# Seven block products in place of eight in the first layer of a second MLP

## Chip, cores and metric

The kernel runs on one core of a Trainium2 chip (trn2). The metric is device time in microseconds of one execution. The kernel before was timed in three runs.

## What is computed

The program is a chain: attention with a cumulative bias (16 heads of 576 tokens and 64 channels), an MLP ("moe"), and a mixture of four MLPs ("moe2"). All is float32. The change lies in the third part:

```python
def _moe2_ref(x, domain_probs, w1, w2):         # x: 1152 x 512, w1: 4 x 512 x 1024, w2: 4 x 1024 x 512
    p = domain_probs / (domain_probs.sum(-1, keepdims=True) + 1e-09)
    out = np.zeros((N, D), dtype=np.float32)
    for e in range(E):
        h = np.maximum(x @ w1[e], 0.0)
        out += p[:, e:e + 1] * (h @ w2[e])
    return out.astype(np.float32)
```

## The kernel before

**Precision.** A float32 operand of the MLPs is held as a pair: `hi`, the value cast to fp32r, and `lo`, the rest. `products` (L150) makes one block product from three matmuls: weight hi by data hi, weight lo by data hi, weight hi by data lo. All of one tile add up in one PSUM bank.

**Stages.** The 1152 tokens lie in three chunks of 512, 320 and 320 (`sizes`). Phases 0, 1 and 2 run the first MLP on a chunk each; attention is woven into phases 0 and 1. Phase 3 runs the four second MLPs on all chunks. Its unit is a block: 4 tiles of 128 hidden channels of one expert, so 8 blocks in all. A block has

- an up part (`up`, L170): for each tile of hidden channels and each chunk one PSUM tile, of 4 steps over the 512 inputs by 3 matmuls. So 4 tiles x 12 matmuls of 512 columns, and 4 x 2 x 12 of 320. ACT writes `hi` of the hidden tile `ht` with Relu (L190), DVE `lo` (L191).
- a down part (`down2`, L216): for each of the 9 tiles of 128 tokens 12 matmuls of 512 columns; DVE scales by the expert's probability and adds to `oacc` (L228). `up` of the next block stands before and behind a block's `down2` (`in_order`, L119).

**Weights** come in pieces of 128x1024 float32 (512 KB): SP loads one into `raw` (4 buffers, `RAW`), ACT casts `hi` (L104), POOL subtracts for `lo` (L105), into one of 4 buffers `w`. The pieces of the first MLP arrive as 64-bit patterns; in phase 0 `convert` (L73) makes float32 of each in the `raw` buffer, with one ACT and four DVE instructions (L84 to L88). In phase 3 a block takes two up pieces and two down pieces.

**What sets the order.** Each engine has one queue, worked off in order. A scheduler that simulates the program places the instructions in it; pools of tiles with a fixed number of buffers hold an instruction back until a buffer is free. PSUM has 8 banks of 512 float32 columns: 3 for the MLPs in phases 0 to 2, 6 in phase 3 (`ps_all`). The outputs `y_t` of the first MLP are split into `hi` and `lo` as their tiles end (L212, L213).

Of the kernel before, what the change touches and what calls it, by code (L numbers as in the profile page):

```python
# [18 lines left out]
def attention_moe_moe2(ctx: ExitStack, tc: tile.TileContext, q, k, v, s, w_in, w_out, probs, w1, w2, out):  # L19
# [21 lines left out]
    RAW, SPLIT = 4, 4  # L41
    sizes = (512, 320, 320)
    starts = (0, 512, 832)

    const = ctx.enter_context(tc.tile_pool(name="const", bufs=1))
    ypool = ctx.enter_context(tc.tile_pool(name="ypool", bufs=1))
    rawp = ctx.enter_context(tc.tile_pool(name="rawp", bufs=RAW))
    xpool = ctx.enter_context(tc.tile_pool(name="xpool", bufs=1))
# [101 lines left out]
    def products(ps, pairs):  # L150

        pairs = [p for (wh, wl), (xh, xl) in pairs for p in ((wh, xh), (wl, xh), (wh, xl))]
        for i, (a, b) in enumerate(pairs):
            nc.tensor.matmul(ps, a, b, start=(i == 0), stop=(i == len(pairs) - 1))  # L154
# [15 lines left out]
    def up(e, chunks, h, tiles):  # L170

        nonlocal w_up
        x = x_t if e is None else y_t
        for i in tiles:
# [6 lines left out]
            for c, to, n in pieces(chunks):  # L181
# [3 lines left out]
                if e is None:  # L185
                    nc.scalar.activation(hi, ps, AF.Prelu, alpha=0.01)
                    nc.scalar.activation(ps, ps, AF.Prelu, alpha=0.01)  # L187
                    nc.vector.tensor_tensor(lo, ps, f32(hi), ALU.subtract)  # L188
                else:
                    nc.scalar.activation(hi, ps, AF.Relu)  # L190
                    nc.vector.scalar_tensor_tensor(lo, ps, 0.0, f32(hi), ALU.max, ALU.subtract)  # L191
                yield

    def down1(f, chunks, h, w):

        for c, to, n in pieces(chunks):
            if f == 0:
                yacc[c] = ypool.tile([P, KD, sizes[0]], F32, tag="yacc", name="yacc")[:, :, : sizes[c]]
            for d in range(KD):
# [4 lines left out]
                if f == 0:  # L204
                    nc.scalar.copy(ya, ps)
                else:
                    nc.vector.tensor_tensor(ya, ps, ya, ALU.add)  # L207
                if f + len(h) == DFF // P:
                    if d == 0:
                        y_t[c] = xpool.tile([P, 2, KD, sizes[c]], F32R, tag=f"x{c}", name=f"y{c}")  # L210
                    hi, lo = at(y_t[c], d)
                    nc.scalar.copy(hi, ya)  # L212
                    nc.vector.tensor_tensor(lo, ya, f32(hi), ALU.subtract)  # L213
# [325 lines left out]
```

## Time and profile before

| | us |
|---|---|
| median of the three timed runs | 762.21 |
| lowest and highest of them | 760.3 and 763.31 |
| span of the profiled execution | 762.5 |
| of it: PE busy | 739.5 (97%) |
| PE weight loads (PEld) busy | 651.3 (85%) |
| DVE busy | 322.3 (42%) |
| ACT busy | 301.9 (40%) |
| POOL busy | 266.1 (35%) |

The profile shows one execution, from its first to its last instruction; its span lies among the three timed runs. PE is TensorE's matmuls, PEld its weight loads, which overlap the matmuls. A row's mean duration is that of one instruction from start to end; neighbouring matmuls overlap, so the pace of a row of matmuls is not its mean but the time of many, less one, over their count. The granted clock of TensorE is 1.00 of full speed (2.4 GHz) from 113 us on.

### The profile page before, as it was taken

To read this page: it belongs to the slowest core of one execution; us is meant where nothing else is said; L and a number is where in the kernel's file an instruction comes from. 1 tells how busy PE (TensorE), PEld (TensorE's weight loads), DVE (VectorE), ACT (ScalarE), POOL (GpSimd) and SP (SyncE) were. 2 spreads that over 40 slices of the span, in tenths; PEclk is the share of its full clock that TensorE was granted. 3 is DMA by queue.
4 is the path that set the end of the run, shared out by engine and by line. 5 is a ranking of instruction groups with operands and counts; after the bars stand their busy time and mean duration, and the time that the engine had idled before them with its cause. 6 is when DMAs were issued, how large, how long until landed. Compare 5 with 4: busy or idle time off the path is not lost.

```text
span 762.5 us, 10790 instructions
## 1 busy us (share of the span) xinstructions
PE 739.5 (97%) x4140; PEld 651.3 (85%) x4140; DVE 322.3 (42%) x665; ACT 301.9 (40%) x613; POOL 266.1 (35%) x198
## 2 busy tenths in 40 slices
PE   7889999989999999999999999999999999999997
PEld 5677778867899999999998888988989889888886
DVE  4889666985564553223322222222222222222222
ACT  4766596565577574654320321212203112032010
POOL 3553164667376353676311221212203121122100
PEclk9789999999999999999999999999999999999999
DMA  7888946765242223445210110201001101010002
GB/s 241 231 254 290 323 155 217 209 217 178 97 142 99 89 84 110 140 139 166 69 41 28 56 56 0 84 28 56 28 28 60 53 32 51 28 28 1 0 29 96
DMA packets 45955, 80.74 MB, mean 106 GB/s; under 512 B 4528, under 2 KB 24496, under 8 KB 45904
## 3 DMA queue, kind: packets, MB, share of 16 engines
q1 hardware_dynamic: 45904, 80.06, 32.8%
q8 instruction: 32, 0.52, 0.3%
q14 instruction: 19, 0.16, 0.1%
HBM read 69.26 MB, written 10.78 MB: 105 GB/s over the span
## 4 chain that ended last, share of the span: by engine, by line
PE 84%; DVE 5%; DMA 5%; issue 2%; ACT 2%; SPq 1%; POOL 0%; ACTq 0%; DVEq 0%
PE ps_d L154 38%; PE ps_u L154 36%; PE ps_o L406 5%; PE ps_pt L397 2%; DMA r<-in_moe_w_out_dram 2%; DMA r<-in_moe_w_in_dram 2%; PE ps_sc L383 2%; PE ps_sc L380 1%; DVE raw L85 1%; DVE raw L88 1%; DMA pn<-in_moe_domain_probs_dram 1%; ACT raw L84 1%; DVE z L384 1%; DVE raw L87 1%; DVE raw L86 0%
## 5 line engine op out<-in xcount | busy, mean ns | idle before, releaser
L105 POOL TENSOR_TENSOR w<-raw,w 128x1024 fp32r<-128x1024 f32 x80 | 195.7, 2456 | 364.4 <-ACT w L104 361.7
L154 PE MATMUL ps_u<-y,w 128*128 128x320 f32 (+1 forms) x1152 | 201.5, 336 | 0.7 <-DVE yacc L207 0.7
L154 PEld LDWEIGHTS ps_u<-y,w 128*128 128x128 f32 x1152 | 185.2, 188 | 17.0 <-ACT w L104 0.9
L154 PE MATMUL ps_d<-w,ht 128*128 128x512 f32 x864 | 197.3, 389 | 0.0
L154 PEld LDWEIGHTS ps_d<-w,ht 128*128 128x128 f32 x864 | 161.9, 188 | 33.2
L104 ACT CAST w<-raw 128x1024 fp32r<-128x1024 f32 x80 | 83.1, 1044 | 170.0 <-issue 161.9
L191 DVE SCALAR_TENSOR_TENSOR ht<-ps_u,ht 128x320 fp32r<-128x320 f32 (+1 forms) x96 | 53.6, 558 | 146.8 <-ACT ht L190 146.8
L154 PE MATMUL ps_u<-x,w 128*128 128x320 f32 (+1 forms) x576 | 112.9, 343 | 1.7 <-DVE ht L188 1.7
L154 PE MATMUL ps_d<-ht,w 128*128 128x320 f32 (+1 forms) x576 | 110.3, 341 | 0.9 <-DVE ht L188 0.9
L190 ACT ACTIVATE ht<-ps_u 128x320 fp32r<-128x320 f32 (+1 forms) x96 | 47.2, 491 | 142.1 <-PE ps_u L154 142.1
L154 PEld LDWEIGHTS ps_u<-x,w 128*128 128x128 f32 x576 | 91.9, 189 | 9.0 <-DVE ht L188 2.3
L228 DVE SCALAR_TENSOR_TENSOR oacc<-ps_d,pn,oacc 128x512 f32<-128x512 f32 x63 | 47.3, 751 | 122.8 <-PE ps_d L154 122.8
L154 PEld LDWEIGHTS ps_d<-ht,w 128*128 128x128 f32 x576 | 92.2, 188 | 7.9 <-DVE ht L188 1.1
L406 PEld LDWEIGHTS ps_o<-vs,pv 128*128 128x128 f32 x480 | 64.4, 200 | 10.6 <-DVE xo L412 3.8
L406 PE MATMUL ps_o<-vs,pv 128*128 128x64 f32 x480 | 65.9, 277 | 3.8 <-DVE xo L412 2.4
L376 POOL TENSOR_SCALAR_AFFINE_SELECT nck<-nck 128x128 f32<-128x128 f32 x80 | 34.1, 441 | 85.8 <-DMA nck<-cum_d 37.7
L388 ACT ACTIVATE z<-z,mn 128x512 f32<-128x512 f32 (+4 forms) x80 | 48.4, 606 | 29.8 <-DVE mn L384 23.7
L384 DVE CUSTOM_DVE_ANT_0 z<-ps_sc,nck 128x512 f32<-128x512 f32 (+4 forms) x80 | 40.8, 511 | 32.1 <-PE ps_sc L383 18.9
L398 ACT COPY pv<-ps_pt 128x512 f32<-128x512 f32 (+3 forms) x96 | 39.2, 422 | 22.6 <-PE ps_pt L397 17.2
L380 PE MATMUL ps_sc<-kr,qz 128*128 128x128 f32 (+4 forms) x96 | 35.9, 470 | 8.3 <-DVE mn L384 7.9
L397 PE MATMUL ps_pt<-ident,z 128*128 128x128 f32 x240 | 42.0, 280 | 1.8 <-ACT pv L398 1.3
L188 DVE TENSOR_TENSOR ht<-ps_u,ht 128x320 fp32r<-128x320 f32 (+1 forms) x48 | 26.4, 553 | 36.0 <-ACT ps_u L187 35.8
(55 smaller groups left out, 440.6 us busy)
## 6 DMA issues: line engine op xcount, KB each, us to landing
raw<-w_f SPq DMA_DIRECT2D x32, 512.0 KB, 3.3
raw<-in_moe_w_dram SPq DMA_DIRECT2D x32, 512.0 KB, 3.5
r<-in_moe_w_in_dram SPq DMA_DIRECT2D x16, 512.0 KB, 6.9
w_f<-raw SPq DMA_DIRECT2D x16, 512.0 KB, 3.7
r<-in_moe_w_out_dram SPq DMA_DIRECT2D x16, 512.0 KB, 5.8
nck<-cum_d SPq DMA_DIRECT2D x8, 576.0 KB, 5.1
vs<-in_v_dram SPq DMA_DIRECT2D x12, 256.0 KB, 4.1
kr<-in_k_dram SPq DMA_DIRECT2D x8, 288.0 KB, 4.5
```

Of the source, the lines that this page charges most:

```text
L104: nc.scalar.copy(w[:, 0], raw)
L105: nc.gpsimd.tensor_tensor(w[:, 1], raw, f32(w[:, 0]), ALU.subtract)
L154: nc.tensor.matmul(ps, a, b, start=(i == 0), stop=(i == len(pairs) - 1))
L190: nc.scalar.activation(hi, ps, AF.Relu)
L191: nc.vector.scalar_tensor_tensor(lo, ps, 0.0, f32(hi), ALU.max, ALU.subtract)
L228: nc.vector.scalar_tensor_tensor(oacc[tt], ps, p, oacc[tt], ALU.mult, ALU.add)
L380: nc.tensor.matmul(ps, self.qz[:, j, own], self.kr[:, keys], start=True, stop=True)
L384: nc.vector.tensor_tensor_reduce(out=z[:, keys], in0=ps, in1=nck[:, j, keys], scale=-(D ** -0.5), scalar=3.0e38 if pc == 0 else mn[:, 0:1] ...
L388: nc.scalar.activation(z, z, AF.Exp, bias=mn[:, pc : pc + 1], scale=-1.0, accum_out=self.st[i][:, j : j + 1])
L397: nc.tensor.transpose(pt[:, (kt - k0) * P : (kt - k0 + 1) * P], z[:, tiles[kt][0] : tiles[kt][2]], ident)
L398: nc.scalar.copy(pv[:, k0:k1].rearrange("p t q -> p (t q)"), pt)
L406: nc.tensor.matmul(o[:, j], pv[:, kt], self.vs[:, kt, j], start=(kt == 0), stop=(kt == i))
```

## The change

The first layer of the second MLPs goes by Strassen's scheme (in Winograd's form). A product of a weight cut into 2x2 blocks (256 inputs by 128 hidden channels each) with tokens cut into 2x2 blocks (256 inputs by n tokens each) needs seven products of sums of blocks and not eight of the blocks. The tokens are paired in two sets: set 0 has the first 256 tokens of chunk 0 beside its last 256 (n = 256), set 1 has chunk 1 beside chunk 2 (n = 320).

- `seven` replaces the split of an up piece: DVE forms four sums of 128x256 in `sums`; ACT and POOL then split seven blocks (1792 columns, in three instructions each) and not four (1024). The two buffers `w7` and the one of `sums` have a pool of their own.
- `paired_tokens` forms the four sums of the token blocks (DVE) and splits seven blocks (ACT and DVE), once for each set, before the first block. `down1` adds the last tile of the first MLP straight into a float32 `y_t`, and no longer splits it.
- `up2` makes one pair of hidden tiles for one set: seven products of 6 matmuls each, into 4 PSUM banks. Three of the four banks are written, read by ACT or DVE, and then added onto by a second product. ACT copies `p1` (L264); DVE adds into `u2`, `u4` and three tiles of `mixed` (L266 to L275); then three Relu and three `lo` (L278, L279), of which two read `mixed` and no longer PSUM.
- `second` sets the order: the down tiles of set 0, one `up2` of the next block, the down tiles of set 1, three more `up2`.
- `RAW` falls from 4 to 3. Down pieces of phase 3 have two buffers (`wdown`), opened with the other pools of phase 3 when those of the first MLP close. PSUM has 8 banks in one pool in phase 3, where it had 6.

```diff
-    RAW, SPLIT = 4, 4
+    RAW, SPLIT = 3, 4
+    sets = (((0, 0), (0, 256), 256), ((1, 0), (2, 0), 320))
...
+    def seven(raw):
+        r = raw.rearrange("p (k f) -> p k f", k=KD)
+        a11, a12, a21, a22 = (r[:, 2 * j : 2 * j + 2, i * P : (i + 1) * P] for i in range(2) for j in range(2))
+        sums = w7pool.tile([P, 4, 2, P], F32, tag="sums", name="sums", bufs=1)
+        nc.vector.tensor_tensor(sums[:, 0], a21, a22, ALU.add)
+        nc.vector.tensor_tensor(sums[:, 1], sums[:, 0], a11, ALU.subtract)
+        nc.vector.tensor_tensor(sums[:, 2], a11, a21, ALU.subtract)
+        nc.vector.tensor_tensor(sums[:, 3], a12, sums[:, 1], ALU.subtract)
+        w = w7pool.tile([P, 2, 7, 2, P], F32R, tag="w7", name="w7", bufs=2)
+        for i, j, of in ((0, 2, r[:, :, :P]), (2, 3, a22), (3, 7, sums.rearrange("p s k f -> p (s k) f"))):
+            hi, lo = (w[:, l, i:j].rearrange("p s k f -> p (s k) f") for l in range(2))
+            nc.scalar.copy(hi, of)
+            nc.gpsimd.tensor_tensor(lo, of, f32(hi), ALU.subtract)
+        return w
...
-    def products(ps, pairs):
+    def products(ps, pairs, onto=False):
...
-            nc.tensor.matmul(ps, a, b, start=(i == 0), stop=(i == len(pairs) - 1))
+            nc.tensor.matmul(ps, a, b, start=(i == 0 and not onto), stop=(i == len(pairs) - 1), skip_group_check=onto)
...
+    def paired_tokens(s, pool):
...
+        nc.vector.tensor_tensor(sums[:, 1], b12, b11, ALU.subtract)
+        nc.vector.tensor_tensor(sums[:, 2], b22, sums[:, 1], ALU.subtract)
+        nc.vector.tensor_tensor(sums[:, 3], b22, b12, ALU.subtract)
+        nc.vector.tensor_tensor(sums[:, 0], b21, sums[:, 2], ALU.subtract)
+        y = y7[s] = pool.tile([P, 2, 7, 2, n], F32R, name=f"y7_{s}")
+        for i, j, of in ((0, 2, left), (2, 3, b22), (3, 7, sums.rearrange("p s k t -> p (s k) t"))):
+            hi, lo = (y[:, l, i:j].rearrange("p s k t -> p (s k) t") for l in range(2))
+            nc.scalar.copy(hi, of)
+            nc.vector.tensor_tensor(lo, of, f32(hi), ALU.subtract)
+
+    def up2(w, s):
...
+        bank = [ps_mm.tile([P, 512], F32, tag="mm", name=f"ps_u{i}")[:, :n] for i in range(4)]
+
+        def product(to, a, b, onto=False):
+            products(bank[to], [(at(w, a, k), at(x, b, k)) for k in range(2)], onto)
+
+        product(0, 0, 0)
+        nc.scalar.copy(p1, bank[0])
+        product(1, 4, 5)
+        nc.vector.tensor_tensor(u2, bank[1], p1, ALU.add)
+        product(2, 3, 4)
+        nc.vector.tensor_tensor(u4, bank[2], u2, ALU.add)
+        product(3, 5, 6)
+        nc.vector.tensor_tensor(mixed[:, 1], bank[3], u4, ALU.add)
+        product(0, 1, 1, True)
+        product(2, 6, 2, True)
+        nc.vector.tensor_tensor(mixed[:, 2], bank[2], u2, ALU.add)
+        product(3, 2, 3, True)
+        nc.vector.tensor_tensor(mixed[:, 0], bank[3], u2, ALU.add)
+        for of, f, cols in ((bank[0], 0, slice(0, n)), (mixed[:, 2], 0, slice(n, 2 * n)), (mixed[:, :2].rearrange("p i t -> p (i t)"), 1, slice(0, 2 * n))):
+            hi, lo = at(ht, f, cols)
+            nc.scalar.activation(hi, of, AF.Relu)
+            nc.vector.scalar_tensor_tensor(lo, of, 0.0, f32(hi), ALU.max, ALU.subtract)
+        return ht
...
+        for i, (e, *_) in enumerate(blocks):
+            wd = next_w(2)
+            down2(e, parts[0], h[i], wd)
+            if i + 1 < len(blocks):
+                up_part(i + 1, 0, 0)
+            down2(e, parts[1], h.pop(i), wd)
+            if i + 1 < len(blocks):
+                for pair, s in ((1, 0), (0, 1), (1, 1)):
+                    up_part(i + 1, pair, s)
...
+        paired_tokens(0, y7p)
         for _ in mlps(phases[2]):
             pass
...
+    paired_tokens(1, y7q)
+    first.close()
+    banks.close()
+    ps_mm = ctx.enter_context(tc.tile_pool(name="ps_all", bufs=8, space=PSUM))
+    wpool = ctx.enter_context(tc.tile_pool(name="wdown", bufs=2))
```

On PE, the up part of one block of phase 3 stands in a row before (`ps_u` is the PSUM tile, `y0` to `y2` the chunks, `w` the weight piece):

```order
L154 MATMUL ps_u_4556<-y0_2231,w_4409 128x512 x12
L154 MATMUL ps_u_4571<-y1_3456,w_4409 128x320 x12
L154 MATMUL ps_u_4586<-y2_4048,w_4409 128x320 x12
L154 MATMUL ps_u_4602<-y0_2231,w_4409 128x512 x12
L154 MATMUL ps_u_4617<-y1_3456,w_4409 128x320 x12
L154 MATMUL ps_u_4632<-y2_4048,w_4409 128x320 x12
```

These are the first two of the block's four hidden tiles. Now, on PE, the same block after the down tiles of set 1 (`y7_0` and `y7_1` are the token sums of the two sets, `ps_u0` to `ps_u3` the four banks of one `up2`):

```order
L177 MATMUL ps_u0_4635<-y7_0_3512,w7_4421 128x256 x6
L177 MATMUL ps_u1_4636<-y7_0_3512,w7_4421 128x256 x6
L177 MATMUL ps_u2_4637<-y7_0_3512,w7_4421 128x256 x6
L177 MATMUL ps_u3_4638<-y7_0_3512,w7_4421 128x256 x6
L177 MATMUL ps_u0_4695<-y7_1_4124,w7_4409 128x320 x6
L177 MATMUL ps_u1_4696<-y7_1_4124,w7_4409 128x320 x3
L177 MATMUL ps_u0_4635<-y7_0_3512,w7_4421 128x256 x6
L177 MATMUL ps_u1_4696<-y7_1_4124,w7_4409 128x320 x3
L177 MATMUL ps_u2_4637<-y7_0_3512,w7_4421 128x256 x6
L177 MATMUL ps_u3_4638<-y7_0_3512,w7_4421 128x256 x6
```

The second products onto banks 0, 2 and 3 stand behind nine or more matmuls of the next `up2`.

On DVE, the rows of the same stretch after the change (`tmp` holds `u2`, `u4` and `mixed`; L266, L268 and L270 free banks 1, 2 and 3 for it):

```order
L266 TENSOR_TENSOR tmp_4634<-ps_u1_4636,tmp_4634 128x256
L268 TENSOR_TENSOR tmp_4634<-ps_u2_4637,tmp_4634 128x256
L270 TENSOR_TENSOR tmp_4634<-ps_u3_4638,tmp_4634 128x256
L266 TENSOR_TENSOR tmp_4694<-ps_u1_4696,tmp_4694 128x320
L279 SCALAR_TENSOR_TENSOR ht_4633<-ps_u0_4635,ht_4633 128x256
L273 TENSOR_TENSOR tmp_4634<-ps_u2_4637,tmp_4634 128x256
L275 TENSOR_TENSOR tmp_4634<-ps_u3_4638,tmp_4634 128x256
L279 SCALAR_TENSOR_TENSOR ht_4633<-tmp_4634,ht_4633 128x256
L268 TENSOR_TENSOR tmp_4694<-ps_u2_4697,tmp_4694 128x320
L279 SCALAR_TENSOR_TENSOR ht_4633<-tmp_4634,ht_4633 128x512
L270 TENSOR_TENSOR tmp_4694<-ps_u3_4698,tmp_4694 128x320
```

Before, only the `lo` of each PSUM tile (L191) stood here. On ACT, the start of phase 3 after the change (`y2` is the last output of the first MLP, `w_4152` and `w_4217` the first two down pieces):

```order
L248 CAST y7_1_4124<-y1_3447 128x1280
L248 CAST y7_1_4124<-y2_4071 128x640
L264 COPY tmp_4156<-ps_u0_4157 128x256
L248 CAST y7_1_4124<-sums_4119 128x2560
L127 CAST w_4152<-raw_4150 128x1024
L278 ACTIVATE ht_4155<-ps_u0_4157 128x256
L127 CAST w_4217<-raw_4215 128x1024
L264 COPY tmp_4221<-ps_u0_4222 128x256
```

The copy that the second `up2` needs (`tmp_4221`) stands behind the cast of the token sums of set 1 and two casts of weights.

## Rows read from the trace of the kernel before

**Rows 1.** Busy time by stretch: start:end, length, then time (count) for each engine

```profile
core 0: us, PE busy (x) PEld busy (x) DVE busy (x) ACT busy (x) POOL busy (x), PEclk, DMA share, GB/s
41.00:113.00 72.00, 66.05 (x397) 52.72 (x396) 54.88 (x148) 49.78 (x118) 29.79 (x38) 0.98 0.78 257
113.00:200.00 87.00, 83.45 (x433) 69.04 (x432) 63.60 (x120) 54.01 (x116) 54.36 (x41) 1.00 0.62 195
...
293.00:362.00 69.00, 68.48 (x469) 68.20 (x468) 21.89 (x44) 37.78 (x69) 46.07 (x20) 1.00 0.46 146
...
399.81:449.33 49.52, 49.52 (x255) 43.34 (x253) 13.46 (x21) 9.88 (x16) 9.56 (x4) 1.00 0.14 43
```

**Rows 2.** PE in order of time: start, length, line, tile, shape, count, [idle before]

```profile
343.71 7.20 PE L154 MATMUL ps_d<-ht,w 128*128 128x320 f32 x48
...
362.15 13.24 PE L154 MATMUL ps_u<-y,w 128*128 128x512 f32 x74 [0.68 <-DVE yacc L207]
...
399.81 24.67 PE L154 MATMUL ps_d<-w,ht 128*128 128x512 f32 x108
424.31 25.18 PE L154 MATMUL ps_u<-y,w 128*128 128x512 f32 x144
449.33 0.86 PE L154 MATMUL ps_d<-w,ht 128*128 128x512 f32 x3
```

**Rows 3.** PE waits from 293 us to the end: us in total, times, longest

```profile
PE ps_u L154 <- DVE yacc L207: 0.7, 1, 0.7
```

**Rows 4.** PE groups by shape: count | busy us, mean ns | idle before

```profile
L154 PE MATMUL ps_d<-w,ht 128*128 128x512 f32 x864 | 197.3, 389 | 0.0
L154 PE MATMUL ps_u<-y,w 128*128 128x320 f32 x768 | 117.7, 309 | 0.0
L154 PE MATMUL ps_u<-y,w 128*128 128x512 f32 x384 | 93.0, 391 | 0.7 <-DVE yacc L207 0.7
```

**Rows 5.** PE in order of time, two fp32r matmuls of 256 columns in attention

```profile
151.37 0.40 PE L383 MATMUL ps_sc<-ks,qs 128*128 128x256 f32 x2
151.60 0.39 PE L154 MATMUL ps_d<-ht,w 128*128 128x512 f32 x1
```

**Rows 6.** Weight loads of phase 3, one line: duration ns min/median/max

```profile
L154 PEld LDWEIGHTS ps_u<-y,w x1152: 187/188/190, 362.1 to 733.6; 128*128 128x128 f32 x192
```

**Rows 7.** DVE groups by shape

```profile
L228 DVE SCALAR_TENSOR_TENSOR oacc<-ps_d,pn,oacc 128x512 f32<-128x512 f32 x63 | 47.3, 751 | 122.8 <-PE ps_d L154 122.8
L191 DVE SCALAR_TENSOR_TENSOR ht<-ps_u,ht 128x320 fp32r<-128x320 f32 x64 | 31.5, 492 | 69.3 <-ACT ht L190 69.3
L191 DVE SCALAR_TENSOR_TENSOR ht<-ps_u,ht 128x512 fp32r<-128x512 f32 x32 | 22.1, 692 | 77.5 <-ACT ht L190 77.5
L429 DVE TENSOR_TENSOR x<-ps_x,x 128x256 fp32r<-128x256 f32 x4 | 1.7, 416 | 0.7 <-ACT x L428 0.7
```

**Rows 8.** ACT groups by shape, and POOL's weight splits of 400 to 747 us

```profile
L104 ACT CAST w<-raw 128x1024 fp32r<-128x1024 f32 x80 | 83.1, 1044 | 170.0 <-issue 161.9 <-PE ps_d L154 6.4 <-DVE raw L88 1.6
L428 ACT CAST x<-ps_x 128x256 fp32r<-128x256 f32 x4 | 1.5, 366 | 2.6 <-PE ps_x L423 2.6
...
L105 POOL TENSOR_TENSOR w<-raw,w 128x1024 fp32r<-128x1024 f32 x26 | 62.2, 2401 | 270.3 <-ACT w L104 270.3
```

**Rows 9.** DVE and POOL in order of time about 362 us; y (L213) has two SBUF inputs

```profile
360.77 0.49 DVE L213 TENSOR_TENSOR y<-yacc,y 128x320 fp32r<-128x320 f32 x1 [0.53 <-ACT y L212]
...
363.07 1.49 DVE L213 TENSOR_TENSOR y<-yacc,y 128x320 fp32r<-128x320 f32 x1 [1.06 <-ACT y L212]
...
361.81 5.02 POOL L105 TENSOR_TENSOR w<-raw,w 128x1024 fp32r<-128x1024 f32 x2 [3.12 <-ACT w L104]
```

**Rows 10.** Busy time on `raw` tiles up to 200 us (DVE, ACT, POOL), and SP's longest wait

```profile
0.00:200.00 200.00, 75.55 (x64) 36.98 (x34) 46.85 (x18) 0.97 0.72 227
...
SPq L94 <- POOL w L105: 320.1, 32, 22.4
```

More of the change, by code (lines that the diff above doesn't have):

```diff
@@ L172, in up @@
         nonlocal w_up
-        x = x_t if e is None else y_t
+        x = x_t
         for i in tiles:
@@ L184, in up @@
                 hi, lo = at(ht, slice(to, to + n))
[L185 to L191, printed above, removed]
+                nc.scalar.activation(hi, ps, AF.Prelu, alpha=0.01)
+                nc.scalar.activation(ps, ps, AF.Prelu, alpha=0.01)
+                nc.vector.tensor_tensor(lo, ps, f32(hi), ALU.subtract)
                 yield
@@ L205, in down1 @@
                     nc.scalar.copy(ya, ps)
-                else:
-                    nc.vector.tensor_tensor(ya, ps, ya, ALU.add)
-                if f + len(h) == DFF // P:
+                elif f + len(h) < DFF // P:
+                    nc.vector.tensor_tensor(ya, ps, ya, ALU.add)
+                else:
                     if d == 0:
[L210 to L213, printed above, removed]
+                        y_t[c] = xpool.tile([P, KD, sizes[c]], F32, tag=f"x{c}", name=f"y{c}")
+                    nc.vector.tensor_tensor(y_t[c][:, d], ps, ya, ALU.add)
@@ L219, in down2 @@
+    def down2(e, tiles, h, w):
+        for tt in tiles:
             ps = ps_mm.tile([P, 512], F32, tag="mm", name="ps_d2")
-            cols = slice(t * P, (t + 1) * P)
-            products(ps, [(at(h[i], cols), at(w[i // 2], i % 2)) for i in range(len(h))])
-            tt = starts[chunks[0]] // P + t
+            s = int(tt * P >= sizes[0])
+            t0 = tt * P - s * sizes[0]
+            products(ps, [(at(h[i // 2][s], i % 2, slice(t0, t0 + P)), at(w[i // 2], i % 2)) for i in range(2 * len(h))])
@@ L228, in down2, with second, up_part @@
                 nc.vector.scalar_tensor_tensor(oacc[tt], ps, p, oacc[tt], ALU.mult, ALU.add)
-            touched[tt] = touched.get(tt, 0) + len(h)
+            touched[tt] = touched.get(tt, 0) + 2 * len(h)
             if touched[tt] == E * F // P:
                 nc.sync.dma_start(out[tt * P : (tt + 1) * P, :], oacc[tt])
-            yield
+    def second(blocks):
+        parts = (range(0, sizes[0] // P), range(sizes[0] // P, NT))
+        w, h = {}, {}
+        def up_part(i, pair, s):
+            if (i, pair) not in w:
+                (w[i, pair],) = next_w(1)
+            h.setdefault(i, ({}, {}))[pair][s] = up2(w[i, pair], s)
+        for pair, s in ((0, 0), (1, 0), (0, 1), (1, 1)):
+            up_part(0, pair, s)
+        for i, (e, *_) in enumerate(blocks):
[7 more added lines that the diff above has]
+                    up_part(i + 1, pair, s)
     def mlps(groups):
@@ L239, in mlps @@
                 yield from up(e, chunks, h, tiles)
-            elif e is None:
+            else:
                 yield from down1(f, chunks, h, next_w(nf // 2))
-            else:
-                yield from down2(e, chunks, h, next_w(nf // 2))
     def moe1(chunks, nf):
@@ L249, in moe2 @@
         return [(e, f, nf, chunks) for e in es for f in range(0, F // P, nf)]
-    phases = [[moe1([c], 4)] for c in range(3)] + [[moe2(range(E), [0, 1, 2], 4)]]
+    phases = [[moe1([c], 4)] for c in range(3)]
+    blocks2 = moe2(range(E), [0, 1, 2], 4)
     for groups in phases:
```

58 lines of the change are left out of this document (38 added, 20 removed).

## Prediction

> **What bounds the kernel now.** I read the busy time by stretch first, then PE in order of time, then what PE waited for. In a whole block of phase 3, 399.81 to 449.33 us, PE is busy for all of its 49.52 us, DVE for 13.5, ACT for 9.9, POOL for 9.6 [rows 1]. Two rows of PE make up that block: 108 down matmuls, then 144 up matmuls, with the next block's down row right behind [rows 2]. From 293 us to the end PE waited once, 0.7 us at the start of phase 3 [rows 3]. So phase 3 is a count of matmuls times their pace, and nothing else is on its path; the work of the other engines counts only where it makes PE wait.
>
> **The pace of a matmul.** A row of equal matmuls gives it: the row's length less one duration, over the count less one. For 512 columns, (24.67 - 0.389) / 107 = 226.9 ns; for 320 columns, (7.20 - 0.31) / 47 = 146.6 ns [rows 2, 4]. The difference is 80.3 ns for 192 columns, 0.418 ns a column, which is the 2.4 GHz level of the granted clock; a fixed 13 ns is left per matmul. For 256 columns the line gives 146.6 - 64 x 0.418 = 119.8 ns. No long row of 256 exists, but attention has pairs: one starts at 151.37 and the next matmul at 151.60, so two took 0.23 us, 115 ns each within the rounding [rows 5]. I take 119.8.
>
> **What the products save.** Removed are 384 matmuls of 512 columns and 768 of 320 [rows 4]: 384 x 226.9 + 768 x 146.6 ns = 87.1 + 112.6 = 199.7 us. (The block's own row agrees: from 424.31 to 449.33 is 25.02 us, times 8 is 200.2 [rows 2].) Added are 16 pairs of hidden tiles x 7 products x 6 matmuls = 672 for each set: 672 x 119.8 + 672 x 146.6 ns = 80.5 + 98.5 = 179.0 us. The saving is **20.7 us**. It is less than the columns alone would give (an eighth of 199.7 is 25.0), since there are 192 more matmuls with 13 ns each, and narrower ones. The down matmuls stay.
>
> **Does the weight load keep that pace?** Every matmul has weights of its own, and a load lasts 188 ns [rows 6], longer than the pace of 146.6. Loads therefore overlap matmuls and each other already. The Trainium skill, "TensorE: Matmul & The Clock Gate", section LDWEIGHTS, puts a load at its columns over 1.2 GHz; for 128 columns that makes an estimate of 107 ns. As a floor under the pace it would lie below 119.8 and change nothing; put in series with the stream it would be the second rival below, worse than priced there. The rows of 320 columns speak against series.
>
> **What DVE, ACT and POOL get, per block.** DVE: five PSUM adds in each of four `up2`, 10 x 0.416 + 10 x 0.492 = 9.1 us, and eight sums of 256 columns for the weights, 8 x 0.416 = 3.3; the `lo` have the same columns as before [rows 7]. That makes 13.5 + 12.4 = 25.9 us. ACT: four copies of `p1` at about 0.4 and 1536 more columns to cast at 1.044 us per 1024 [rows 8], 9.9 + 3.2 = 13.1. POOL: the same columns at 2.401 per 1024 [rows 8], 9.6 + 3.6 = 13.2. The new block is 49.5 - 2.6 = 46.9 us long, so DVE is at 55%, the others below 30%. None becomes the bound by its share. I cost all of it at nothing in the steady state, and this is the cover: the second product onto a bank needs the bank read. By the order on PE, between the first product of bank 3 and its second there stand 12 matmuls of 320 and 12 of 256 columns, 1.76 + 1.44 = 3.2 us, while DVE owes three adds of 0.42, two of them begun earlier. If the cover is gone, PE waits by what DVE is late beyond 3.2 us.
>
> The new buffers: the down pieces' two buffers come free when the set 1 tiles end, and three `up2` follow, 5.0 + 6.2 + 6.2 = 17.4 us, against two casts and two POOL splits, 1.0 + 2 x 2.4 = 6 us. A `w7` buffer is refilled (POOL 1792 columns, 4.2 us, and ACT ahead of it) while one `up2` and four down tiles run, 6.2 + 48 x 0.2269 = 17.1 us. Both cost nothing.
>
> **Start of phase 3.** Now PE waits 0.7 us there [rows 2]; that stays. New is that set 1's sums need the last output of the first MLP. Count from that output. DVE then owes the rest of four sums of 640 columns and two `lo` of 1280 and 640; by 1.04 ns a column from the two L191 rows [rows 7] about 5.7 us. Only then can ACT cast the 2560 columns of sums (2.6 us), and behind that in ACT's queue stand two weight casts (1.04 each), a Relu and the `p1` copy of the second `up2`: done at about 11.2 us. PE reaches the product that needs this copy after 66 matmuls of 256 columns and 6 of 320, 8.8 us, at 0.7 + 8.8 = 9.5. So PE waits about 1.8 us. Bounds: 0, if the first sums and casts run while the last down tiles do; 6.6, if both of POOL's first down splits also hold DVE up (below). I take **+2.0**.
>
> **Phase 2.** Set 0's sums, its `lo` and the first two weight pieces add to DVE some 6.9 + 3.3 us, where it is busy 21.9 of 69 [rows 1]. Three PSUM banks of 12 x 0.1466 = 1.76 us each leave a lead of 3.5 us; the longest single piece, a `lo` of 2048 columns (2.2 us) behind one POOL split (2.4), overshoots it by 1.1 once. Bounds 0 and 2; I take **+0.5**. What `down1` no longer splits is hidden now and frees nothing.
>
> **`raw` with three buffers.** SP's loads wait for `raw` buffers for 320 us in all [rows 10], but these waits lie behind PE's work: the pieces are needed later. In phase 0 a conversion takes DVE 75.55 / 16 = 4.7 us [rows 10] and now starts one piece later. PE is idle 6.0 and 3.6 us in 41 to 113 and 113 to 200 us [rows 1], so there are gaps to grow or shrink. The scheduler also places attention's work there a little differently. Bounds -1 and one conversion, +4.7; I take **+0.5**.
>
> **Sum.** 762.5 - 20.7 + 2.0 + 0.5 + 0.5 = 744.8 us against the profiled span, which lies 0.3 above the median of the runs; so **744.5 us**. The tail is the same nine down tiles.
>
> **Rival 1, slower: DVE queues behind POOL.** A DVE instruction with two SBUF inputs waits for a POOL instruction under way: the `y` of 320 columns that takes 0.49 us took 1.49 at 363.07 [rows 9], beside POOL's splits. The Trainium skill, "SBUF — State Buffer", section "Who interferes with whom", has this as a rule: the two share a read interface, and whichever comes second is blocked until the first ends. The trace agrees, with those 1.49 us. The change makes two of three `lo` in each `up2` such instructions (they read `mixed`), and the eight weight sums. The place is DVE's L279 in the three `up2` that follow the set 1 tiles, where POOL splits the down pieces: behind a blocked L279 stand L268 and L270, for which PE's second products wait. POOL's splits of a block are 13.2 us, the longest 2.4; one of these is inside the 3.2 us of cover, two in a row are not. Slower by over 0.5% (3.8 us) needs (20.7 - 3.0 + 3.8) / 8 = 2.7 us of waiting per block; at 1 us for each `up2`, 4 per block, it is 744.5 + 32 = 777 us. Against: by the order the down splits run while PE makes the first products, before the first `lo` from `mixed`; adds that read PSUM have one SBUF input. The milder form, 1 us per block, gives 753.
>
> **Rival 2, no change: loads set the pace of the narrow matmuls.** If no long row can go below the 146.6 ns of today's narrowest, the 672 matmuls cost 672 x 26.8 ns = 18 us more: 762.5. For it: no row of more than two shows 256 columns, and loads last 188 ns. Against: the pairs [rows 5], and the equal 13 ns at both widths.
>
> **Rival 3: start uncovered.** The 6.6 us in place of 2.0 gives 749; inside the range.
>
> **How the numbers follow.** The forecast with its terms between their bounds, 739 to 751: 0.68. Milder waiting on DVE, 751 to 757: 0.14. No change (rival 2, or about 2 us of waiting per block): 0.06. Slower (rival 1): 0.08. Below 739 (earlier phases gain by another order): 0.04. The range is 739 to 757 and leaves 0.18 out. A measurement of this kernel can tell about 0.5%, 3.8 us, from no change: faster 0.86, same 0.06, slower 0.08.
>
> **What would show it.** Right: the row of 24 `ps_u` matmuls of 256 columns lasts about 2.9 us plus an overlap; the block from down row to down row is 46.9 us; the only PE waits of phase 3 lie in its first 15 us and add up to about 2 us. Wrong in the pace: such a row nears 3.6 us. Wrong in the cover: PE waits for L268, L270 or L264 in every block, with L279 behind POOL on DVE at over 1.5 us. Wrong in the early phases: the first matmul of phase 3 moves by more than 3 us from 362.15.

## The result, and the profile after

The changed kernel takes 752.61 us (median of four runs, 751.41 to 754.1) against 762.25 before (median of four runs by now): a ratio of 0.987, 95% interval 0.984 to 0.990. So it is faster, by 9.6 us and not by the 17.7 that the prediction named; the time lies inside its range (739 to 757) and 8 us above its point.

The span of the profiled execution is 749.6 us (its time: 751.41; every run of this study lists a time 1.7 to 2.1 us above its span). Busy time by stretch of the changed kernel, with the columns of [rows 1]:

```profile
293.00:367.78 74.78, 68.62 (x465) 67.58 (x464) 35.97 (x57) 38.96 (x67) 51.79 (x23) 1.00 0.40 134
403.01:449.99 46.98, 46.98 (x277) 42.64 (x276) 26.55 (x53) 13.14 (x24) 14.93 (x8) 1.00 0.15 46
```

The last line is a whole block of phase 3: PE busy throughout, 46.98 us long, against 49.52 in [rows 1]. The line above it is the one that went wrong: phase 2 lasts to 367.78, with 6 us of idle PE, where in [rows 1] PE was idle for 0.5. What PE waited for from 293 us to the end, in the changed kernel (total, times, longest):

```profile
PE ps_d L177 <- DVE ht L210: 3.3, 1, 3.3
PE ps_d L177 <- DVE y L230: 2.0, 1, 2.0
PE ps_u L177 <- ACT tmp L264: 1.3, 1, 1.3
```

The fourth and last is 0.7 us before phase 3; [rows 3] had that one alone. PE in order of time, changed kernel:

```profile
304.79 2.02 PE L177 MATMUL ps_d<-ht,w 128*128 128x320 f32 x12 [2.04 <-DVE y L230]
...
356.26 1.19 PE L177 MATMUL ps_d<-ht,w 128*128 128x320 f32 x7
360.76 6.27 PE L177 MATMUL ps_d<-ht,w 128*128 128x320 f32 x41 [3.31 <-DVE ht L210]
367.78 9.02 PE L177 MATMUL ps_u<-y,w 128*128 128x256 f32 x72 [0.75 <-issue]
378.06 11.54 PE L177 MATMUL ps_u<-y,w 128*128 128x320 f32 x78 [1.26 <-ACT tmp L264]
...
403.01 3.03 PE L177 MATMUL ps_u<-y,w 128*128 128x256 f32 x24
```

The first long wait stands at the end of phase 1, the second near the end of phase 2. The token sums and weight sums that the prediction costs under "Phase 2" lie on DVE about both; below, "phase 2" means that stretch, from 293 to 367.78 us. From 400 us on PE waits for nothing.

**Where the time is.** The 673rd matmul of the first MLP starts at 287.3 us (before: 288.0), so the two profiled executions are level there. The first matmul of phase 3 starts 5.6 us later than in [rows 2]; the two waits are 5.3 of that. From that 673rd matmul it is 80.5 us to the first of phase 3 (before: 74.2), 6.3 more. From the first matmul of phase 3 to the end it is 749.6 - 367.8 = 381.8 us, before 762.5 - 362.15 = 400.35: 18.5 us less. Sum: -0.7 + 6.3 - 18.5 = -12.9, which is the difference of the two spans.

**What held DVE.** DVE in order of time, changed kernel, about both waits:

```profile
298.68 0.69 DVE L241 TENSOR_TENSOR sums<-y 128x512 f32<-128x512 f32 x1 [0.21 <-PE ps_x L513]
299.29 2.91 DVE L243 TENSOR_TENSOR sums<-y 128x512 f32<-128x512 f32 x1
...
356.33 2.57 DVE L112 TENSOR_TENSOR sums<-raw 128x256 f32<-128x256 f32 x1 [2.82 <-POOL w L120]
358.82 1.48 DVE L114 TENSOR_TENSOR sums<-raw 128x256 f32<-128x256 f32 x1
360.23 0.48 DVE L210 TENSOR_TENSOR ht<-ps_u,ht 128x320 fp32r<-128x320 f32 x1
```

and POOL in the same stretches:

```profile
298.98 2.67 POOL L128 TENSOR_TENSOR w<-raw,w 128x1024 fp32r<-128x1024 f32 x1 [1.61 <-ACT w L127]
...
356.25 2.37 POOL L128 TENSOR_TENSOR w<-raw,w 128x1024 fp32r<-128x1024 f32 x1
358.58 2.31 POOL L120 TENSOR_TENSOR w<-raw,w 128x512 fp32r<-128x512 f32 x2
```

L241 and L243 have the same shape: 0.69 us with POOL idle, 2.91 with a split of POOL begun 0.31 us ahead. L112 took 2.57 us here and 0.42 on average in phase 3. The `lo` of the last hidden tile (L210), for which the eighth of PE's 48 down matmuls waits and all behind it, stands in DVE's queue behind L112 and L114. This is the mechanism of the prediction's first rival, and of the Trainium skill, "SBUF — State Buffer", section "Who interferes with whom"; but in phase 2, where the prediction had given it 0.5 us, and not in the blocks of phase 3.

That left the theory to test. **Theory A:** DVE's instructions with two SBUF inputs are held up by POOL's splits, and this makes both waits of phase 2. **Theory B:** the 3.3 us come from the single buffer of `sums` (L112 had been idle for 2.82 us for it). **Theory C:** DVE has too much work there, wherever POOL is.

### The profile page after: what moved, and what is told of

Same layout as the page of the kernel before. It is cut to its first block, busy times and chain, and to the rows that moved or that the text cites. A ratio compares the mean times of both kernels' runs of the same rounds, so it can differ in the third digit from the quotient of the medians.

```text
span 749.6 us, 11518 instructions
## 1 busy us (share of the span) xinstructions
PE 720.3 (96%) x4332; PEld 647.0 (86%) x4332; DVE 439.2 (59%) x891; ACT 328.4 (44%) x671; POOL 309.4 (41%) x230
## 4 chain that ended last, share of the span: by engine, by line
PE 78%; DVE 7%; DMA 5%; issue 4%; POOL 3%; ACT 2%; SPq 1%; POOLq 0%; DVEq 0%; ACTq 0%
PE ps_d L177 36%; PE ps_u L177 32%; PE ps_o L496 5%; PE ps_pt L487 2%; PE ps_sc L473 2%; DMA r<-in_moe_w_in_dram 2%; DMA nck<-cum_d 1%; POOL w L128 1%; DMA qr<-in_q_dram 1%; DVE y L249 1%; DVE raw L90 1%; PE ps_sc L470 1%; DVE raw L92 1%; DMA kr<-in_k_dram 1%; POOL w L120 1%
## 5 line engine op out<-in xcount | busy, mean ns | idle before, releaser
L128 POOL TENSOR_TENSOR w<-raw,w 128x1024 fp32r<-128x1024 f32 x64 | 158.9, 2495 | 213.5 <-ACT w L127 210.3
L177 PE MATMUL ps_d<-w,ht 128*128 128x512 f32 x864 | 203.4, 390 | 0.0
L177 PE MATMUL ps_u<-y,w 128*128 128x256 f32 (+1 forms) x1344 | 186.1, 296 | 2.1 <-ACT tmp L264 1.3
L177 PEld LDWEIGHTS ps_d<-w,ht 128*128 128x128 f32 x864 | 160.0, 188 | 31.5
L127 ACT CAST w<-raw 128x1024 fp32r<-128x1024 f32 x64 | 66.7, 1045 | 80.8 <-PE ps_d L177 68.7
L466 POOL TENSOR_SCALAR_AFFINE_SELECT nck<-nck 128x128 f32<-128x128 f32 x80 | 36.0, 465 | 86.9 <-DVE mn L474 36.4
L120 POOL TENSOR_TENSOR w<-raw,w 128x512 fp32r<-128x512 f32 (+1 forms) x32 | 34.3, 1092 | 80.5 <-ACT w L119 74.6
L278 ACT ACTIVATE ht<-tmp 128x256 fp32r<-128x256 f32 (+1 forms) x64 | 35.8, 564 | 53.7 <-DVE tmp L273 48.6
L279 DVE SCALAR_TENSOR_TENSOR ht<-tmp,ht 128x256 fp32r<-128x256 f32 (+1 forms) x64 | 51.3, 808 | 9.7 <-ACT ht L278 9.4
L120 POOL TENSOR_TENSOR w<-sums,w 128x1024 fp32r<-128x1024 f32 x16 | 46.0, 2877 | 2.5 <-ACT w L119 2.5
## 6 DMA issues: line engine op xcount, KB each, us to landing
kr<-in_k_dram SPq DMA_DIRECT2D x8, 288.0 KB, 5.4
```

Source lines behind the costliest of these rows:

```text
L120: nc.gpsimd.tensor_tensor(lo, of, f32(hi), ALU.subtract)
L177: nc.tensor.matmul(ps, a, b, start=(i == 0 and not onto), stop=(i == len(pairs) - 1), skip_group_check=onto)
L279: nc.vector.scalar_tensor_tensor(lo, of, 0.0, f32(hi), ALU.max, ALU.subtract)
L466: nc.gpsimd.affine_select(nck[:, j, a:kw], nck[:, j, a:kw], [[-1, P]], ALU.is_ge, MASKED, 0, 1)
```

## Experiments

**The changed kernel again** (no edit; the neighbour of the next three).

> The changed kernel again, as the measure for the runs beside it. Theory A (DVE's instructions with two SBUF inputs queue behind POOL near the end of phases 1 and 2 and hold up what PE waits for) and theory B (the single buffer of the weight sums holds DVE up) both expect 751 to 754 us, with PE waiting about 2 us for y and 3 us for ht between 295 and 362 us.

Measured: 752.32 us (751.26 to 757.88), ratio 0.990 [0.985, 0.994]. The waits are the same, 3.2, 2.0 and 1.3 us. But something else differs. PE in order of time, this execution:

```profile
360.02 7.80 PE L177 MATMUL ps_d<-ht,w 128*128 128x320 f32 x41 [3.19 <-DVE ht L210]
```

and its busy time by stretch, with the granted clock as the third number from the end:

```profile
360.00:362.00 2.00, 1.98 (x10) 1.98 (x11) 1.26 (x3) 1.05 (x1) 0.15 (x1) 0.76 0.53 204
362.00:364.00 2.00, 2.00 (x9) 2.00 (x9) 0.14 (x1) 0.00 (x0) 1.96 (x1) 0.50 0.79 269
```

The same 41 matmuls last 7.80 us, where they lasted 6.27 in the first execution at a granted clock of 1.00. Behind the wait the clock is at 0.50, its lower level (1.2 GHz), and the wait of 3.2 us costs 1.5 us more than itself. After 366 us it is at 1.00 again.

**Two buffers for the weight sums.**

```diff
-        sums = w7pool.tile([P, 4, 2, P], F32, tag="sums", name="sums", bufs=1)
+        sums = w7pool.tile([P, 4, 2, P], F32, tag="sums", name="sums", bufs=2)
```

> The weight sums get two buffers in place of one, nothing else. Theory B: the second piece's first sum no longer waits 2.8 us for POOL's reading of the first piece's sums; the 3.3 us that PE waits for ht in phase 2 goes, and the time falls by about 3 us against the changed kernel. Theory A: the sums start earlier but stand behind POOL's splits all the same (1.4 to 2.6 us for a sum that takes 0.42 alone); PE still waits 2 us or more there, and the time falls by 1.5 us at most.

Measured: 752.84 us (752.51 to 755.61), as the neighbour. DVE in order of time:

```profile
354.95 0.42 DVE L112 TENSOR_TENSOR sums<-raw 128x256 f32<-128x256 f32 x1
355.29 2.64 DVE L114 TENSOR_TENSOR sums<-raw 128x256 f32<-128x256 f32 x1
357.86 2.58 DVE L113 TENSOR_TENSOR sums<-sums,raw 128x256 f32<-128x256 f32 x1
360.47 1.37 DVE L115 TENSOR_TENSOR sums<-raw,sums 128x256 f32<-128x256 f32 x1
361.76 0.48 DVE L210 TENSOR_TENSOR ht<-ps_u,ht 128x320 fp32r<-128x320 f32 x1
```

The sums no longer wait for the buffer; L112 is through in 0.42 us, and now L114, L113 and L115 are stretched, one behind each of POOL's splits. PE's wait is 3.4 us. Theory B falls.

**The weight sums on POOL.**

```diff
-        nc.vector.tensor_tensor(sums[:, 0], a21, a22, ALU.add)
+        nc.gpsimd.tensor_tensor(sums[:, 0], a21, a22, ALU.add)
...
```

(all four sums of `seven`)

> The four sums of each weight piece are made on POOL, before its splits on the same queue, and no longer on DVE. Theories A and B alike: PE's 3.3 us of waiting for ht in phase 2 goes, so about 3 us less than the changed kernel; under A the 2 us wait for y at the end of phase 1 stays, since the token sums are still on DVE. A third reading (PE's wait has another cause, such as ACT's order) expects the wait to stay. POOL gets about 5 us more work per block of phase 3, which should cost nothing there (at most 31% busy before).

Measured: 752.36 us (749.06 to 754.54), as the neighbour. PE's waits from 290 us to the end:

```profile
PE ps_u L177 <- DVE tmp L266: 3.9, 1, 3.9
PE ps_d L177 <- DVE y L230: 2.0, 1, 2.0
```

The wait of 3.3 us in phase 2 is gone, and phase 3 starts at 362.9 us. But POOL's work now reaches into the start of phase 3, and there the token sums of set 1 queue behind it: L241 lasts 2.98 us and L244 2.97, where 640 columns take 0.81 with POOL idle (L243 at 368.67 in the changed kernel). PE waits 3.9 us for L266 behind them, and the granted clock is 0.71 on average from 366 to 376 us. From its first matmul to the end phase 3 lasts 386.6 us, 4.8 more than in the changed kernel. What was won in phase 2 was given back in phase 3.

**The token sums of set 0 later.** They start when four hidden tiles of phase 2 are made, so that the `y` of phase 1 (L230) no longer stand behind them.

```diff
...
-        paired_tokens(0, y7p)
-        for _ in mlps(phases[2]):
-            pass
+        for i, _ in enumerate(mlps(phases[2])):
+            if i == 3:
+                paired_tokens(0, y7p, hs_last[-4:])
```

> The token sums of set 0 are held back: each starts behind one of the first four hidden tiles of phase 2, by four copies of one column on DVE that the sums overwrite. Theory A: the 2.0 us that PE waits for y at the end of phase 1 goes, the 3.3 us in phase 2 stay, so 1.5 to 2 us less than the changed kernel; up to 1 us of new waiting is possible at the start of phase 2. If the wait for y comes from the end of attention and not from the token sums, it stays and the time is that of the changed kernel.

Measured: 756.92 us (751.8 to 758.23), 4.6 more than the neighbour by the medians: the 1.5 to 2 us did not come. The size of the loss is open, since its ratio to the kernel before, 0.992 [0.989, 0.995], overlaps the neighbour's. PE's waits from 290 us to the end, first line:

```profile
PE ps_d L177 <- DVE ht L212: 6.5, 2, 3.7
```

The wait for `y` is gone, but the sums now stand ahead of the hidden tiles' `lo`: L250 took 2.36 us and L251 2.75 (0.69 alone), behind POOL. A held-up instruction that is moved holds up others.

**POOL's splits on DVE, from phase 2 to the end** (first) **and only for 18 pieces** (second: those of phase 2 and the first two up pieces of phase 3).

```diff
+    def rest():
+        return nc.vector if len(ready) >= 32 else nc.gpsimd
...
-            nc.gpsimd.tensor_tensor(lo, of, f32(hi), ALU.subtract)
+            rest().tensor_tensor(lo, of, f32(hi), ALU.subtract)
...
-        nc.gpsimd.tensor_tensor(w[:, 1], raw, f32(w[:, 0]), ALU.subtract)
+        rest().tensor_tensor(w[:, 1], raw, f32(w[:, 0]), ALU.subtract)
```

In the second, `32 <= len(ready) < 50`. This gives DVE more work, and takes away what it may be blocked by: theories A and C say opposite things.

> The same for all weight pieces from phase 2 on, so POOL is idle in phase 3 as well. DVE gets about 6 us more per block of 46.9 us but no waiting behind POOL. Theory A: as the run beside it, and the 1.3 us wait at the start of phase 3 stays or falls; about 747 us. Theory C: DVE at about 70% lets PE wait in every block, 755 us or more.

> The lo half of the weight pieces of phase 2 and of the first two up pieces of phase 3 (18 pieces) is subtracted on DVE in place of POOL. POOL then has nothing to do from about 298 to 372 us; DVE gets 18 instructions of 1.1 to 1.9 us more. Theory A (sums queue behind POOL on the shared read interface): the waits of 2.0 us for y and 3.3 us for ht go, no sum lasts longer than its own 0.4 to 0.7 us, and the time falls to about 747 us. Theory C (DVE has too much work there, whoever else runs): about 22 us more DVE work in 70 us make the waits grow, to 754 us or more.

Measured: 748.18 us (747.83 to 748.75), ratio 0.982 [0.980, 0.985], for all pieces; 746.91 us (745.91 to 749.13), ratio 0.981 [0.978, 0.984], for 18. Busy time in phase 2, first of the changed kernel:

```profile
298.00:367.78 69.78, 63.62 (x430) 62.59 (x429) 34.77 (x54) 36.31 (x62) 47.42 (x21) 1.00 0.41 137
```

and of the kernel with 18 pieces on DVE:

```profile
298.00:362.26 64.26, 61.77 (x418) 61.01 (x417) 46.13 (x72) 34.76 (x60) 0.00 (x0) 1.00 0.45 142
```

DVE is busy for 46.13 of 64.26 us (72%) where it was for 34.77 of 69.78 (50%), POOL for none. The stretch is 5.5 us shorter, but the two executions are not level at 298 us: this one has 418 matmuls left in it and the other 430. From the 673rd matmul of the first MLP to phase 3 it is 76.5 us against 80.5, so 3.9 us are the change's here. On DVE the second token sum (L246 here, L243 in the changed kernel), in order of time:

```profile
297.70 0.69 DVE L246 TENSOR_TENSOR sums<-y 128x512 f32<-128x512 f32 x1
```

It takes 0.69 us where it took 2.91. PE's waits from 290 us to the end, kernel with 18 pieces on DVE:

```profile
PE ps_u L180 <- ACT tmp L267: 1.6, 1, 1.6
PE ps_d L180 <- DVE y L233: 0.9, 1, 0.9
PE ps_u L180 <- issue: 0.8, 1, 0.8
PE ps_u L180 <- DVE ht L213: 0.7, 1, 0.7
```

Theory C falls: DVE has taken over 18 pieces at 1.22 us or more, some 22 us, and its queue moves faster. Its busy time rose by 11 us only, since POOL no longer stretches its other instructions. Theory A holds for the wait of 3.3 us, which is gone, and for 1.1 of the 2.0. The other 0.9 us for `y` stand with POOL idle, and a wait of 0.7 us is new (L213, at 310 us): POOL makes neither, and both names point to DVE's own queue. A split of 1024 columns takes DVE 1.22 us and POOL 2.40 or more.

**One product less.** The second product of bank 0 is left out in every `up2`.

```diff
-        product(0, 1, 1, True)
```

> The second product of the seven (block 1 by block 1, onto bank 0) is left out, so the output is not the reference's. If phase 3 is the count of matmuls times their pace, 32 x 6 matmuls less give 96 x 119.8 + 96 x 146.6 ns = 25.6 us less in phase 3 (381.8 to 356.2 us from its first matmul to the end). If the work of DVE, ACT or POOL is about to bind, PE begins to wait in the blocks and it is 5 us short of that or more.

Measured: one run, 728.81 us; phase 3 lasts 358.7 us from its first matmul, 23.1 less than 381.8, and PE waits for nothing after 400 us. Without that product PE is earlier at the banks of the start and waits there 3.2 us (2.1, 0.8 and 0.3 in place of 1.3). Counting these, the products are worth 25.0 of the 25.6 expected.

**Half of the banks in phase 3.**

```diff
-    ps_mm = ctx.enter_context(tc.tile_pool(name="ps_all", bufs=8, space=PSUM))
+    ps_mm = ctx.enter_context(tc.tile_pool(name="ps_all", bufs=4, space=PSUM))
```

> Phase 3 has four PSUM buffers in place of eight, so one up2 can no longer stand beside another or beside down tiles: the cover of DVE's adds is taken away. If the cover is what hides the five PSUM adds and the lo, PE waits in each up2 for about the chain behind its last product (an add of 0.42, Relu, lo, then the next product), 2 us or more in 32 up2: 60 us or more longer. If DVE's adds would be hidden anyway, under 10 us.

Measured: one run, 755.2 us. PE in order of time, four banks:

```profile
367.28 3.83 PE L177 MATMUL ps_u<-y,w 128*128 128x256 f32 x30 [0.75 <-issue]
372.24 3.19 PE L177 MATMUL ps_u<-y,w 128*128 128x256 f32 x24 [1.13 <-DVE tmp L266]
377.53 4.61 PE L177 MATMUL ps_u<-y,w 128*128 128x256 f32 x24 [2.09 <-DVE tmp L275]
382.84 1.42 PE L177 MATMUL ps_u<-y,w 128*128 128x256 f32 x9 [0.71 <-DVE tmp L268]
```

Waits stand at the start of phase 3 alone; it lasts 386.1 us from its first matmul, 4.3 more. Of these, 2.7 are waits (1.13, 2.09 and 0.71 in place of 1.26); 1.6 are the clock, which fell to 0.50 behind the wait of 2.09: the row of 24 took 4.61 us, and 3.03 at 1.00. The steady blocks are untouched, by the busy time of 400 to 735 us with four banks:

```profile
400.00:735.00 335.00, 335.00 (x1960) 303.57 (x1959) 190.55 (x341) 91.11 (x165) 95.27 (x53) 1.00 0.13 40
```

1960 matmuls in 335 us, with PE busy throughout as with eight banks. But the run did not take the whole cover away, as the expectation assumed. PE in a steady block, four banks:

```profile
406.75 3.75 PE L177 MATMUL ps_u<-y,w 128*128 128x256 f32 x30
410.34 2.92 PE L177 MATMUL ps_d<-w,ht 128*128 128x512 f32 x12
413.11 1.59 PE L177 MATMUL ps_u<-y,w 128*128 128x256 f32 x12
```

Behind the first 30 matmuls of this `up2` (four first products and the second onto bank 0) a down tile stands before the second products onto banks 2 and 3. In the next `up2`, at 425.46, six matmuls of 320 columns of the `up2` behind it stand there. So other matmuls of 0.9 us or more still stand between the two products, and the run does not show what happens with none.

**Three `raw` buffers in the kernel before.**

```diff
-    RAW, SPLIT = 4, 4
+    RAW, SPLIT = 3, 4
```

> The kernel before with one change: three raw buffers in place of four. The prediction gave this term +0.5 us with bounds -1 and +4.7; the traces so far (the first 288 us of the changed kernel are 0.65 us shorter than those of before) say that it costs nothing. So my theory expects the kernel before within 1 us (ratio 1.000, between 0.9985 and 1.0015). The rival, that the three buffers do cost a few us in phase 0 and that the changed kernel wins them back by another order of its instructions, expects +2 to +5 us.

Measured: 762.18 us (ten runs) against 762.51 for the kernel before (thirteen): ratio 1.0002 [0.998, 1.002]. The buffer costs nothing that can be measured, within 1.8 us either way.

**A buffer of its own for the token sums,** on top of the 18 pieces on DVE.

```diff
-        sums = scratch.tile([P, 4 * 2 * 320], F32, tag="scratch", name="sums")...
+        sums = scratch.tile([P, 4 * 2 * 320], F32, tag="scratch", name="sums", bufs=1)...
...
-        tmp = scratch.tile([P, 4 * 2 * 320], F32, tag="scratch", name="tmp")[:, : 6 * n]...
-        p1, u2, u4, mixed = tmp[:, 0], tmp[:, 1], tmp[:, 2], tmp[:, 3:]
+        tmp = scratch.tile([P, 5 * 320], F32, tag="tmp", name="tmp")[:, : 5 * n]...
+        p1, u2, u4, mixed = tmp[:, 0], tmp[:, 1], tmp[:, 3], tmp[:, 2:]
```

> The kernel of dvelo2 once more, as the neighbour of dvelo2t on the same chip: about 747 us, ratio 0.981, and four short PE waits between 298 us and the end that add up to about 4 us (1.6 of them ACT tmp L267).

> dvelo2 with the token sums in a buffer of their own and two buffers for tmp alone (in dvelo2 the second up2 of phase 3 gets the buffer of the token sums of set 1, so its copy of p1 waits until the last lo of those sums, 2.83 us on DVE, has read them; to make room u4 is overwritten in place, five tiles in tmp and not six). Theory D: the wait for ACT tmp at the start of phase 3 is this one buffer; then it falls from 1.6 to below 0.5 us and the time by 1 to 1.6 us against dvelo2b. Theory E: what holds the copy back is the place of its neighbours in the queues of ACT (two weight casts) and DVE (the lo of 2560 columns), as the prediction had it; then the wait moves to another name (DVE tmp L269 or ACT tmp L267) and the time stays within 0.5 us of dvelo2b.

Measured: 747.78 us (746.38 to 749.82, ratio 0.980 [0.976, 0.984]) without the buffer and **744.93 us** (743.19 to 747.59), ratio 0.977 [0.973, 0.981], with it. The waits of the first are those of the run before, but for 1.9 us in place of 0.8 ahead of phase 3. PE in order of time with it, then ACT:

```profile
363.28 18.22 PE L180 MATMUL ps_u<-y,w 128*128 128x256 f32 x138 [1.20 <-issue]
```

```profile
367.14 0.37 ACT L267 COPY tmp<-ps_u 128x256 f32<-128x256 f32 x1 [2.44 <-PE ps_u L180]
368.23 2.34 ACT L251 CAST y<-sums 128x2560 fp32r<-128x2560 f32 x1 [0.72 <-DVE sums L247]
```

The wait for `tmp` is gone (138 matmuls in one row), and phase 3 lasts 380.0 us from its first matmul, against 382.2 of its neighbour and 381.8 of the changed kernel. This is what theory D expected, but the run does not tell D from E: with the buffer free, the copy of the second `up2` (367.14) also got another place, ahead of the token sums' cast and of both weight casts in ACT's queue. In the timed runs the gain of 2.9 us lies within overlapping intervals, so its size is open. Both versions beat the changed kernel; this one is the fastest complete kernel of the study.

## Why the prediction was right or wrong

**Pace of a matmul of 256 columns: right.** The row of 24 at 403.01 gives (3.03 - 0.283) / 23 = 119.4 ns, with 0.283 us the mean of one (changed kernel, groups by shape, the line that answers to [rows 4]); the forecast was 119.8. Rival 2 is out.

```profile
L177 PE MATMUL ps_u<-y,w 128*128 128x256 f32 x672 | 88.1, 283 | 0.8 <-issue 0.7
```

**The saving: right.** Phase 3 from its first matmul to the end became 18.5 us shorter, forecast -20.7 with +2.0 at the start: 18.7. A block is 46.98 us, forecast 46.9. That the products count with their pace shows in the run with one product less: 25.0 us of 25.6.

**The other engines' work per block: right, but for POOL.** DVE 26.55 us (25.9), ACT 13.14 (13.1), POOL 14.93 (13.2). POOL's splits of four sums take 2.88 us on average, against the 2.40 of [rows 8]:

```profile
L120 POOL TENSOR_TENSOR w<-sums,w 128x1024 fp32r<-128x1024 f32 x16 | 46.0, 2877 | 2.5 <-ACT w L119 2.5
```

**Rival 1 in the blocks: the blocking is there, the wait is not.** The `lo` from `mixed` of 640 columns takes 1041 ns in the changed kernel and 819 with no POOL work in phase 3. DVE's groups by shape, 400 to 735 us, in the changed kernel (count | busy us, mean ns | idle before):

```profile
L279 DVE SCALAR_TENSOR_TENSOR ht<-tmp,ht 128x640 fp32r<-128x640 f32 x15 | 15.6, 1041 | 4.6 <-ACT ht L278 4.6
```

and the same view of the kernel with all splits on DVE, where L279 is L282:

```profile
L282 DVE SCALAR_TENSOR_TENSOR ht<-tmp,ht 128x640 fp32r<-128x640 f32 x15 | 12.3, 819 | 0.8 <-ACT ht L281 0.8
```

But PE waits for none of it. That it costs nothing was right, and so was what the prediction held against this rival: the down splits run while PE makes first products, and the adds that PE needs read PSUM. In the changed kernel POOL splits both down pieces of a block in a row, and DVE's adds L268 and L270 fall into that time:

```profile
421.72 4.78 POOL L128 TENSOR_TENSOR w<-raw,w 128x1024 fp32r<-128x1024 f32 x2 [19.25 <-ACT w L127]
```

```profile
424.06 0.42 DVE L268 TENSOR_TENSOR tmp<-ps_u,tmp 128x256 f32<-128x256 f32 x1 [0.23 <-PE ps_u L177]
424.78 0.42 DVE L270 TENSOR_TENSOR tmp<-ps_u,tmp 128x256 f32<-128x256 f32 x1 [0.29 <-PE ps_u L177]
```

With one input from PSUM they take 0.42 us beside POOL, where a weight sum of the same shape with two SBUF inputs took 2.57. How much of the 3.2 us of cover was needed no run shows; the run with four banks left less of it, and the blocks kept their pace.

**Start of phase 3: size right, cause only half.** PE waits 1.3 us (and 0.75 in place of 0.7 before its first matmul), forecast 2.0. The prediction put it down to the copy's place in ACT's queue behind two weight casts. ACT in order of time, changed kernel:

```profile
375.85 1.03 ACT L127 CAST w<-raw 128x1024 fp32r<-128x1024 f32 x1
377.61 0.37 ACT L264 COPY tmp<-ps_u 128x256 f32<-128x256 f32 x1 [0.73 <-DVE y L249]
```

Behind the second cast ACT is idle for 0.73 us, until DVE's last `lo` has read the token sums of set 1: their buffer is the one that the second `tmp` gets. Without that wait the copy would be through 0.73 us earlier. So 0.7 of the 1.3 us are the buffer, which the prediction did not have, and about 0.5 are the queue. That the sum of both came near 2.0 is in part luck.

**Phase 2: the step that failed.** Forecast +0.5 with bounds 0 and 2; in the profiled execution it is 5.3 us of waits, and the first matmul of phase 3 moved by 5.6 us, over the 3 that the prediction had named as a sign of being wrong here. Of the waits, 3.7 us went when POOL was idle. Three things were wrong in that step. It took a lead of 3.5 us from three PSUM banks; but a row of down matmuls needs the `lo` of the hidden tile just made, and PE had only 7 matmuls, 1.19 us, before it needed L210. It took the longest single instruction (a `lo` of 2048 columns) for the danger; the small sums, of 0.42 and 0.69 us by themselves, grew to 2.57 and 2.91, since what each waits for is POOL's instruction and not its own size. And it let this happen once, where POOL works for 47 of 70 us in that stretch and three sums in a row were held up in the run with two `sums` buffers. The row that told it was at hand, the 1.49 us of [rows 9]; beyond that one split it was weighed for phase 3 alone, where POOL is busy for 15 of 47 us.

**The number: inside the range by a way that the prediction did not name.** 752.61 lies in the part from 751 to 757 us that it gave a chance of 0.14 as "milder waiting on DVE", and beside its 753 for 1 us per block. But no block waits. The blocking came in phase 2, so that this price fits is luck. Nor do the terms' own bounds add up to the 739 to 751 that got 0.68: with 0 to 6.6, 0 to 2 and -1 to 4.7 they give 740.5 to 754.8.

**What PE's wait costs beyond itself: not in the sum.** Behind the wait of about 3 us in phase 2 the granted clock fell to 0.50 in some executions: the 41 matmuls took 7.80 us in the second execution and 8.72 with two `sums` buffers, 6.27 where it stayed at 1.00. The first profile of the changed kernel was one without the fall, and the fastest of its four runs.

**`raw`: right.** Forecast +0.5, measured within 1.8 us of nothing.

**Span and median: compared wrongly, without harm to the point.** The prediction set the profiled span beside the median of the times. A time is 1.8 us above its span, so the profiled execution of before was one of about 764.3 us, 2 above the median, and the first one of the changed kernel was 1.2 below its own: 12.9 us between the two spans are 9.6 between the medians. The forecast difference, 17.7 us, came off the median, so the point stands as it was meant. The 9.6 are 18.5 less 5.3 (waits of phase 2), less 1.5 (the clock, as in the second execution), less about 2 that lie before phase 2 or in the spread of the runs (the ratio's interval is 2.2 us either way); these 2 us stay open. Two executions of one kernel can differ by more ahead of phase 2: with 18 pieces on DVE, the 673rd matmul of the first MLP started at 285.7 us in one and at 288.3 in the other.

## What to carry to other kernels

Before work is added to an engine, look at what stands behind it in that engine's queue and at what its neighbour at the same memory is doing: a small DVE instruction with two SBUF inputs can cost as much as the POOL instruction that it meets, and POOL's share of the stretch hints at how often it meets one. Where DVE has room, taking over POOL's elementwise work can make DVE's queue move faster: 18 weight splits moved to DVE made this kernel about 5 us faster, 3.7 of them PE waits. When PE's time is counted in matmuls, count a wait on PE with what may come behind it, the time at the lower clock.

## What the hardware showed unexpectedly

- The clock behind a wait. After PE waits of 3.19, 3.21, 3.44, 3.68 and 3.9 us (five runs) the granted clock fell to 0.50 for some us; after waits of 3.31 and 3.17 us (the changed kernel, and the one with four banks), at the same place of the program as the first four, it stayed at 1.00. It also fell behind shorter ones: 2.09 us at the start of phase 3 with four banks, and 2.04 us for `y` with two `sums` buffers, where 12 matmuls took 2.50 us in place of 2.02. The Trainium skill, "TensorE: Matmul & The Clock Gate", section "HAM oscillation — how this bites in real kernels", says that a wait which breaks up PE's work can bring the lower clock back; these runs agree, and two executions of the changed kernel show that it differs: 1.5 us in one, nothing in the other.
- POOL slows as well. Its split of 1024 columns took 2.40 us in phase 3 before the change [rows 8] and 2.88 on average for the sums after it.
- Many added matmuls of 256 columns, each with weights of its own, keep 119.4 ns though a weight load lasts 188 [rows 6], and 189 on average in the changed kernel.
